# Linear attention and two gated layers on one core: a planner's durations, one new rule of order, and new urgencies

## The chip, the cores and the metric

The kernel runs on one core of a Trainium2 chip. The metric is the device time of one execution in microseconds (us), from the launch to the end of the one program; the median of several executions is quoted. PE is the tensor engine (PEld its weight loads), DVE the vector engine, ACT the scalar engine, SP the engine whose queue issues the DMAs.

## The reference

Three stages follow each other: a linear attention with complex decays (4 batches, 8 heads, 768 tokens, 48 channels a head), a first layer (3072 tokens, 384 to 2048 to 384, with x * sigmoid(1.702 x)), and a second, gated layer (384 to 1536 to 384).

```python
scale = np.minimum(mag, 0.999) / (mag + 1e-06)        # mag = |a|, a = a_re + i a_im
for t in range(S):
    S_re, S_im = ar*S_re - ai*S_im + k_t v_t^T, ar*S_im + ai*S_re
    y[:, :, t] = einsum('bhd,bhde->bhe', q[:, :, t], S_re)
x = y laid out as (tokens, 384)
h = x @ w_in;  x = (h * sigmoid(1.702 h)) @ w_out
g = x @ w_gate;  out = (g * sigmoid(g) * (x @ w_val)) @ w_out2
```

## The kernel before, in words

The attention is done in chunks of 128 tokens; a unit is two chunks of one batch, and there are 12 units. For each unit DVE and ACT compute the decays, their products over the chunk, and the queries and keys with the decays in them. These go to DRAM (tiles dq and dk) and come back with the heads in the partitions (tiles sq and sk). Then PE makes, for each chunk, the scores (sc, 16 products of 128 columns, in two groups of four heads), the results (y, two groups of four heads, line 592 and, from a batch's second chunk on, line 594: products of 48 columns), the change of the state (ds, line 611, 48 columns) and transposes (kt and xp). Units of a batch depend on each other through the state M.

The unit's result xt feeds the first layer: 16 blocks of 128 hidden channels, for each a step of nine products of 256 columns into h (lines 786 to 788), the activation on ACT (line 839 and 841), the rest gs on DVE (line 847), and LAG = 3 blocks later a step of nine such products into acc. These steps of nine are the wide products of the change. All three kinds of wide products are done in three passes, with each operand split in a high and a low part. The second layer works on blocks of 512 tokens with products of 512 and 384 columns (pg, pv and o).

The weights are float64 in DRAM. For each of the 32 blocks of w_in and w_out a row of steps loads the words (line 733), flags the range on ACT (lines 742 and 745), shifts and joins the bits on DVE (lines 750, 753 and 756), rounds to the high part on ACT (line 768), and takes the low part with two products on PE (lines 773 and 774) and a copy on ACT (line 776).

The order of all instructions on all engines is made by a planner at build time (class Plan). Each strand of work is a generator that asks for its next step with an engine and an estimated duration. Plan.run keeps a time at which each engine falls free, takes the steps that could start within 0.02 us of the earliest one, and among them the one with the smallest urgency number; a still more urgent step for the same engine goes first if it could start within a short time (NEAR) of it. The urgency of a step is URGENCY of its kind, plus ten times the unit's place, plus EXTRA for that unit and kind; the weights have W_FIRST + 2 f W_STEP (w_in) and W_FIRST + (2 f + LAG) W_STEP (w_out); the wide products of the first layer have 1000 for all units. A step on ACT that needs another table of functions than the loaded one has TURN added to its urgency. The planned times decide the order alone; on the chip every engine runs its instructions in that order and waits on semaphores.

The kinds of work have letters: a loads the decays' inputs, l loads q, k and v, d the decays, r their root, p the products, k the keys, i the inverse that the keys take (lines 312 and 313), q the queries, s the loads of sq and sk, t the transposes of the keys, h the heads (y and ds), m the scores, x the transposes of the results, g the activations of the first layer.

Of the kernel before, what the change touches and what calls it, by code (L numbers as in the profile page):

```python
# [15 lines left out]
DRAM = bass.MemoryType.DRAM  # L16
# [14 lines left out]
class Slots:  # L31
    """Places for tiles of one tag, with the times at which they fall free."""
# [5 lines left out]
class Plan:  # L38
    """Puts rows of steps in one order for all engines.

    A row (a generator) asks for what its next step needs: (engine, us), an Event, or Slots; it is
    resumed, and then issues the step. Of the steps that could start first, the one of the most
    urgent row is taken. The times are estimates and only the order rests on them.
    """

    # from the end of a step to the start of one that waits for it
    LAT = {"PP": 0.0, "VP": 0.25, "AP": 0.25, "PV": 0.2, "VV": 0.13, "AV": 0.14, "PA": 0.2, "VA": 0.13, "AA": 0.22}
    # some durations (and those of transfers) are taken long: the order then has slack for them
    SLACK = {"A": 1.05, "V": 1.03}

    def __init__(self):
        self.free = dict(P=0.0, V=0.0, A=0.0, S=0.0, D=0.0)
        self.rows = []
        self.now = 0.0
        self.n = 0
        self.warm = 0.0
        self.table = None
        self.row = [0, 0, None, [], None, "S", NEAR]

    def add(self, urgency, gen, after=False, near=None):  # L60
        """A row: its urgency, number, generator, what its next step waits for, that step, and its last step's engine."""
        row = [urgency, self.n, gen, [(self.now, self.row[5])] if after else [], None, "S",
               near or NEAR]
        self.n += 1
        self.rows.append(row)
        self.advance(row, next(gen, None))
# [17 lines left out]
    def rush(self, by):  # L84
        """Makes the row at work more urgent."""
        self.row[0] -= by

    def need(self, nc, table):
        """At the issue of an activation: the table of functions it takes."""
        if self.table != table:  # L90
            nc.scalar.preload_act_table_set(table)
            self.table = table

    def load(self, event, size):
        """After the issue of a transfer of so many bytes."""
        self.free["D"] = max(self.free["D"], self.now + 0.6) + size * 1.3 / 360e3
        self.set(event, self.free["D"] + 3.1 - self.now)
# [9 lines left out]
    def run(self, until=None):  # L107
        while self.rows and (until is None or until.time is None):
# [3 lines left out]
            ready = []  # L112
            for row in self.rows:
                if isinstance(row[4], tuple):
                    turn = row[4][2:] and row[4][2] != self.table
# [6 lines left out]
            if near:  # L122
                row = min(near, key=lambda x: x[1:3])[3]
            engine, us = row[4][:2]
            us *= self.SLACK.get(engine, 1.0)
            # a table of functions is loaded ahead of the step
            start = self.ready(row, SWITCH if row[4][2:] and row[4][2] != self.table else 0.0)
            if engine == "P":
                # the tensor engine's clock is at half speed after a pause
                if start - self.free["P"] > (0.5 if start < self.warm else 2.0):  # L130
                    self.warm = start + 3.4
                if start < self.warm:
                    us *= 2
            self.free[engine] = self.now = start + us
# [5 lines left out]
def vec(n):  # L140
    return "V", 0.065 + n / 960
# [6 lines left out]
def act2(n, *table):  # L148
    """Two, the second on what the first gave."""
    return "A", 0.44 + n / 600, *table  # L150


def pe(n):
    return "P", n


ISSUE = ("S", 0.48)
NEAR = 0.094
SWITCH = 1.3
TURN = 1018.0  # L160
NEAR0 = [0.129, 0.005]
# [3 lines left out]
class Attention:  # L165
    """Linear attention with complex decays, in chunks of 128 tokens.

    With P[t] the product of a chunk's decays up to t, times the phase of all that came before it
    in the batch, q[t] * P[t] and k[s] / P[s] give the chunk's scores by one product, and the state
    passes from chunk to chunk by real factors (powers of two near the chunk's decay; the phase  # L170
    takes up the rest). A unit is a few chunks of a batch. Channels (h, d) lie in the partitions, in
    NT tiles.
    """
# [24 lines left out]
    def start(self, units):  # L198
        """The rows of work of all units: (batch, first chunk, chunks)."""
# [18 lines left out]
    # ---- loads  # L218
# [29 lines left out]
    # ---- decays: a / (|a| + 1e-6) * min(|a|, 0.999)  # L248
    def decays(self, u):
# [11 lines left out]
        # (the logarithm's domain is 2 ** -64 to 2 ** 64)  # L261
# [32 lines left out]
    def root(self, u):  # L294
        """Of the decays' squares."""
        yield u.ev["m2"]
        yield self.slots["r"]
        yield act2(u.F, LN_EXP)
        self.plan.need(self.nc, LN_EXP)
        u.r = self.tile("r", [128, self.NT, u.T])  # L300
        self.nc.scalar.activation(u.r, u.m2, AF.Ln)
        self.nc.scalar.activation(u.r, u.r, AF.Exp, scale=-0.5)
        self.plan.set(u.ev["root"])

    def inverse(self, u):
        """Of the products' squares."""
# [9 lines left out]
    # ---- products of the decays over the chunk  # L316
    def cmul(self, out, x, y, shape):
        """out = x * y over complex pairs [128, 2, *shape] (x and y may be broadcast)."""
# [13 lines left out]
        else:  # L332
            full = [128, 2, 2] + list(shape)
            yield vec(4 * n)
# [12 lines left out]
    def products(self, u, last):  # L347
# [8 lines left out]
        # over the blocks of eight: in fours, then over the fours  # L356
# [13 lines left out]
        # G[.., c] is the phase at the start of chunk c of the unit  # L370
# [10 lines left out]
        # the product up to the start of each block of eight  # L381
# [8 lines left out]
        # joined with the products within the blocks  # L390
# [16 lines left out]
    def passed_on(self, u, G):  # L407
        """The state's factors mag = 1 / kap, powers of two near the unit's decays; the next unit's first phase."""
# [107 lines left out]
    # ---- the heads of a chunk  # L516
# [3 lines left out]
    def turns(self, u):  # L520
        """The keys with the tokens in the partitions."""
# [4 lines left out]
        for c in range(u.n):  # L526
# [3 lines left out]
            for e in range(2):  # L530
                yield slots["m"]
                yield pe(0.36)
# [15 lines left out]
    def masked(self, u, c, g, at):  # L548
        """Scores of four heads, without those that look ahead."""
# [5 lines left out]
        yield pe(0.87)  # L555
# [11 lines left out]
    def heads(self, u, last):  # L567
# [9 lines left out]
        for c in range(u.n):  # L577
# [5 lines left out]
            for g in range(2):  # L583
# [3 lines left out]
                yield pe(0.79 if first else 1.66)  # L587
# [15 lines left out]
            if not final:  # L603
                yield u.turned[c]
                yield slots["m"]
                yield pe(1.29)
# [37 lines left out]
    def turn_x(self, u, c, ysb, turned):  # L644
        """The tokens as columns, in two parts for the products that follow."""
        nc, slots, plan, HD, NT = self.nc, self.slots, self.plan, self.HD, self.NT
        yield slots["m"]
        yield pe(0.38)
# [17 lines left out]
# a unit's urgency is ten times its place, and for each kind of its work:  # L666
URGENCY = dict(a=717.8, d=595, p=-974.9, r=624.6, i=67.1, q=-855.6, k=-193.2, t=-1225.3, h=-1091.9, g=-676.3, s=781.7, l=1191.9, m=-1725.3, x=-1117.4)
RUSH = 1342.0
RUSH2 = 152.5
# [586 lines left out]
```

## Time and profile before

| | |
|---|---|
| median of 3 executions | 1169.94 us |
| lowest and highest | 1165.85 and 1174.10 us |
| span of the profiled execution, first to last instruction | 1167.8 us |
| PE busy | 1096.8 us (94% of the span) |
| DVE busy | 728.8 us (62%) |
| ACT busy | 554.0 us (47%) |

The profiled execution shows its span alone; its own device time is not listed apart from the three. The span is 2.1 us under the median of the three executions and inside their range. A page of the profile gives the busy time of each engine, then the span in 40 equal slices of 29.2 us (each digit the busy share in tenths, 9 for 90% or more; PEclk is the granted TensorE clock, 9 for nearly or fully 2.4 GHz and 5 for half of it).

### The profile page before, as it was taken

The numbers are of one execution on the slowest core, as the hardware profiler recorded it, in microseconds if no ns is written. First come the engines' busy times: TensorE is split into PE (matmuls) and PEld (weight loads), VectorE is DVE, ScalarE is ACT, GpSimd is POOL, SyncE is SP. The second block draws the span as 40 slices with busy tenths as digits, with TensorE's granted clock in tenths as the row PEclk, the third lists the DMA queues.
The fourth block names the chain that finished last, engine by engine and source line by source line (L and its number), as shares of the span: only waits on it lengthen the run. The fifth ranks groups of instructions, "written<-read, shape, count | busy, mean of one in ns | idle before, by whom it ended". The sixth has DMA issues, their size and how long they took to land.

```text
span 1167.8 us, 18608 instructions
## 1 busy us (share of the span) xinstructions
PE 1096.8 (94%) x7312; PEld 1015.9 (87%) x7312; DVE 728.8 (62%) x1638; ACT 554.0 (47%) x1279; POOL 1.1 (0%) x8
## 2 busy tenths in 40 slices
PE   1549899999999999999999999999999999999996
PEld 0228889999999999999999999888888888888886
DVE  6999988889788998888862599622231231322221
ACT  7987545667447656644442699422121121211211
POOL 0000000000000000000000000000000000000000
PEclk9569999999899999999999999999999999999999
DMA  9770715618257263525813664001010010000000
GB/s 329 251 162 15 164 54 136 159 46 150 82 136 135 70 123 95 122 56 109 163 58 72 211 221 145 27 2 54 1 55 1 1 55 1 28 1 1 28 1 30
DMA packets 101391, 103.54 MB, mean 89 GB/s; under 512 B 14001, under 2 KB 95410, under 8 KB 101298
## 3 DMA queue, kind: packets, MB, share of 16 engines
q1 hardware_dynamic: 101298, 102.29, 34.8%
q8 instruction: 59, 0.97, 0.3%
q14 instruction: 34, 0.28, 0.1%
HBM read 73.95 MB, written 28.32 MB: 88 GB/s over the span
## 4 chain that ended last, share of the span: by engine, by line
PE 86%; DMA 7%; DVE 4%; ACT 2%; issue 1%; SPq 0%; DVEq 0%; ACTq 0%
PE h L786 6%; PE h L788 5%; PE h L787 5%; PE acc L786 5%; PE acc L787 5%; PE acc L788 5%; PE o L1005 4%; PE o L1006 4%; PE o L1007 4%; PE pg L787 4%; PE pv L787 4%; PE pv L786 4%; PE pg L788 4%; PE pg L786 4%; PE pv L788 4%; PE sc L559 4%
## 5 line engine op out<-in xcount | busy, mean ns | idle before, releaser
L975 DVE TENSOR_TENSOR s<-s,pv 128x512 f32<-128x512 f32 x72 | 49.5, 687 | 236.0 <-PE pv L788 234.9
L786 PE MATMUL h<-xt,w 128*128 128x256 f32 x576 | 170.0, 295 | 7.8 <-ACT g L841 6.4
L786 PE MATMUL acc<-gs,w 128*128 128x256 f32 x576 | 169.0, 293 | 0.0
L787 PE MATMUL h<-xt,w 128*128 128x256 f32 x576 | 164.8, 286 | 0.6 <-DVE xt L661 0.6
L787 PE MATMUL acc<-gs,w 128*128 128x256 f32 x576 | 164.5, 286 | 0.4 <-DVE gs L847 0.4
L788 PE MATMUL h<-xt,w 128*128 128x256 f32 x576 | 164.5, 286 | 0.0
L788 PE MATMUL acc<-gs,w 128*128 128x256 f32 x576 | 164.5, 286 | 0.0
L839 ACT ACTIVATE gs<-h 128x256 fp32r<-128x256 f32 x192 | 73.8, 384 | 148.7 <-PE h L788 147.3
L972 ACT ACTIVATE s<-pg 128x512 f32<-128x512 f32 x72 | 43.0, 598 | 174.4 <-PE pg L788 174.4
L786 PEld LDWEIGHTS h<-xt,w 128*128 128x128 f32 x576 | 111.8, 194 | 10.8 <-ACT g L841 8.3
L787 PEld LDWEIGHTS h<-xt,w 128*128 128x128 f32 x576 | 111.9, 194 | 1.0 <-DVE xt L661 1.0
L786 PEld LDWEIGHTS acc<-gs,w 128*128 128x128 f32 x576 | 111.9, 194 | 0.7
L787 PEld LDWEIGHTS acc<-gs,w 128*128 128x128 f32 x576 | 111.8, 194 | 0.7 <-DVE gs L847 0.6
L788 PEld LDWEIGHTS h<-xt,w 128*128 128x128 f32 x576 | 111.8, 194 | 0.0
L847 DVE TENSOR_TENSOR gs<-g,gs 128x256 fp32r<-128x256 f32 x192 | 80.6, 421 | 49.8 <-ACT g L841 48.8
L788 PEld LDWEIGHTS acc<-gs,w 128*128 128x128 f32 x576 | 111.6, 194 | 0.0
L980 ACT CAST p<-s 128x512 fp32r<-128x512 f32 x72 | 44.7, 621 | 130.5 <-DVE s L975 130.5
L1005 PE MATMUL o<-w,p 128*128 128x384 f32 x288 | 97.2, 338 | 0.0
L1006 PE MATMUL o<-w,p 128*128 128x384 f32 x288 | 97.2, 337 | 0.0
L1007 PE MATMUL o<-w,p 128*128 128x384 f32 x288 | 97.1, 337 | 0.0
L787 PE MATMUL pg<-xs,w 128*128 128x512 f32 x216 | 85.1, 394 | 0.0
L787 PE MATMUL pv<-xs,w 128*128 128x512 f32 x216 | 84.7, 392 | 0.0
(128 smaller groups left out, 2448.9 us busy)
## 6 DMA issues: line engine op xcount, KB each, us to landing
words<-in_moe_w_out_dram SPq DMA_DIRECT2D x28, 384.0 KB, 8.4
dq<-qh SPq DMA_DIRECT2D x24, 384.0 KB, 8.9
dk<-p SPq DMA_DIRECT2D x24, 384.0 KB, 6.9
sq<-dq SPq DMA_DIRECT2D x24, 384.0 KB, 7.2
sk<-dk SPq DMA_DIRECT2D x24, 384.0 KB, 8.5
words<-in_moe_w_in_dram SPq DMA_DIRECT2D x16, 384.0 KB, 8.4
p<-in_a_re_dram SPq DMA_DIRECT2D x12, 384.0 KB, 3.8
p<-in_a_im_dram SPq DMA_DIRECT2D x12, 384.0 KB, 4.7
```

Of the source, the lines that this page charges most:

```text
L559: T.matmul(sc[:, h], u.sk[:, 4 * g + h, cols(c)], u.sq[:, 4 * g + h, cols(c)], start=True, stop=True)
L786: T.matmul(out, w[:, 0, ws], xh, start=start, stop=False)
L787: T.matmul(out, w[:, 0, ws], xl, start=False, stop=False)
L788: T.matmul(out, w[:, 1, ws], xh, start=False, stop=stop)
L839: A.activation(gs[:, 0], h, AF.Gelu_apprx_sigmoid)
L847: V.tensor_tensor(out=gs[:, 1], in0=g, in1=gs[:, 0].bitcast(F32), op=ALU.subtract)
L972: A.activation(s, gv[0], AF.Silu)
L975: V.tensor_tensor(out=s, in0=s, in1=gv[1], op=ALU.mult)
L980: A.copy(p2[:, 0], s)
L1005: T.matmul(os[i], p2[:, 0, cols(i)], w[:, 0], start=f == 0, stop=False)
L1006: T.matmul(os[i], p2[:, 0, cols(i)], w[:, 1], start=False, stop=False)
L1007: T.matmul(os[i], p2[:, 1, cols(i)], w[:, 0], start=False, stop=f == F2 - 1)
```

## The change

The dataflow, the tiles, the engines of all steps and the number of instructions of each kind stay. Changed are the planner and its numbers, so that the same steps are issued in another order.

- Two groups of products are marked as thin: y (line 592 and 594) and ds (line 611). The planner sums the time of thin steps that follow each other on PE in `few`. If the step it has picked is thin and `few` and this step come over FEW - 0.6 = 2.3 us, it takes in its place the most urgent other PE step that isn't thin and could start within 0.5 us, if there is one.
- The planner's clock of PE is modelled anew: before, half speed for 3.4 us after a pause; now, in fixed stretches of the planned time, half speed in a stretch that follows one with little work, thin steps counted at 0.2.
- Durations: a wide step of nine products 9 (N / 2400 + 0.0135) for 9 N / 2400 + 0.045 (1.08 for 1.00 us at 256 columns); y 1.79 for 1.66 us, ds 1.36 for 1.29, scores 0.90 for 0.87, transposes 0.33 for 0.36 and 0.38, one form of the complex product on DVE 0.3 us longer.
- All urgencies are new numbers: URGENCY, RUSH, RUSH2, EXTRA, NEAR0, W_FIRST, W_STEP and SPILL.

```diff
-            # a table of functions is loaded ahead of the step
-            start = self.ready(row, SWITCH if row[4][2:] and row[4][2] != self.table else 0.0)
+            if row[4][3:] and self.few and self.few + row[4][1] > FEW - 0.6:
+                other = [x for x in ready if x[3][4][0] == "P" and not x[3][4][3:] and x[0] < start + 0.5]
+                if other:
+                    row = min(other, key=lambda x: x[1:3])[3]
...
             if engine == "P":
-                if start - self.free["P"] > (0.5 if start < self.warm else 2.0):
-                    self.warm = start + 3.4
-                if start < self.warm:
+                self.stretch(start)
+                if self.cold:
                     us *= 2
+                thin = row[4][3:]
+                self.few = (self.few if start - self.free["P"] < 0.3 else 0.0) + us if thin else 0.0
+                at = start
+                while at < start + us:
+                    self.stretch(at)
+                    end = min(start + us, (self.part + 1) * STRETCH)
+                    self.work += (end - at) * (0.2 if thin else 1.0)
+                    at = end + 1e-9
...
+    def stretch(self, at):
+        while self.part < int(at / STRETCH):
+            self.cold = self.work < 0.35 * STRETCH
+            self.part += 1
+            self.work = 0.0
...
-            yield vec(4 * n)
+            yield vec(4 * n, 0.3 if n > 48 else 0.0)
...
-                yield pe(0.79 if first else 1.66)
+                yield thin(0.9 if first else 1.79)
...
-                yield pe(1.29)
+                yield thin(1.36)
...
-                yield pe(9 * N / 2400 + 0.045)
+                yield pe(9 * (N / 2400 + MM))
...
+MM = 0.0135
+FEW = 2.9
+STRETCH = 3.413
-NEAR0 = [0.129, 0.005]
+NEAR0 = [0.122, 0.054]
-URGENCY = dict(a=717.8, d=595, p=-974.9, r=624.6, i=67.1, q=-855.6, k=-193.2, t=-1225.3, h=-1091.9, g=-676.3, s=781.7, l=1191.9, m=-1725.3, x=-1117.4)
-RUSH = 1342.0
-RUSH2 = 152.5
+URGENCY = dict(a=717.8, d=727.2, p=-1381.2, r=1320.1, i=1140.8, q=-1417.6, k=-215.1, t=-1308.3, h=-1078.4, g=-1116.1, s=713.6, l=499.3, m=-1658.9, x=-848.6)
+RUSH = 1467.1
+RUSH2 = 315.3
-W_FIRST, W_STEP = 284.7, 16.205
+W_FIRST, W_STEP = 231.0, 8.038
-SPILL = 450.8
+SPILL = 223.6
```

EXTRA has 12 entries, one a unit. Of the first two, the terms that the prediction names: unit 0 a -2878.5, l -411.4, i 214.5 before and a -1741.1, l -876.9, i 961.2 now; unit 1 a -467.2, i -1245.3 before and a -355.5, i 2394.5 now.

## Rows read from the trace of the kernel before

**Rows 1.** The page: busy time, then the span in 40 slices.

```profile
PE 1096.8 (94%) x7312; PEld 1015.9 (87%) x7312; DVE 728.8 (62%) x1638; ACT 554.0 (47%) x1279; POOL 1.1 (0%) x8
PE   1549899999999999999999999999999999999996
DVE  6999988889788998888862599622231231322221
PEclk9569999999899999999999999999999999999999
```

**Rows 2.** Busy time by stage: PE, PEld, DVE, ACT, POOL, clock, DMA share, GB/s.

```profile
0.00:84.20 84.20, 33.28 (x64) 15.14 (x64) 70.71 (x173) 71.81 (x200) 1.14 (x8) 0.68 0.83 250
84.20:142.56 58.36, 53.81 (x392) 48.66 (x392) 55.93 (x142) 38.19 (x87) 0.00 (x0) 0.96 0.44 97
142.56:600.00 457.44, 450.99 (x3777) 447.18 (x3778) 395.77 (x951) 256.95 (x556) 0.00 (x0) 0.97 0.49 107
716.00:1160.00 444.00, 442.72 (x2134) 390.10 (x2132) 134.36 (x220) 114.31 (x217) 0.00 (x0) 1.00 0.05 18
```

**Rows 3.** The same columns in short stretches around a lower clock.

```profile
139.93:143.35 3.42, 1.50 (x12) 1.33 (x12) 1.90 (x6) 0.59 (x2) 0.00 (x0) 0.97 0.94 243
143.35:146.76 3.41, 3.41 (x15) 2.96 (x15) 2.27 (x7) 0.51 (x1) 0.00 (x0) 0.53 0.03 11
...
197.95:201.37 3.42, 3.42 (x33) 3.42 (x31) 3.39 (x5) 1.79 (x3) 0.00 (x0) 0.97 0.00 0
201.37:204.78 3.41, 3.41 (x18) 3.41 (x18) 2.43 (x8) 2.50 (x4) 0.00 (x0) 0.53 0.00 0
...
300.34:303.76 3.42, 3.42 (x20) 3.42 (x19) 1.74 (x2) 1.24 (x4) 0.00 (x0) 0.50 0.00 0
303.76:307.17 3.41, 3.41 (x21) 3.41 (x21) 1.62 (x4) 0.48 (x1) 0.00 (x0) 0.53 0.02 5
...
631.40:634.82 3.42, 3.42 (x20) 3.42 (x19) 0.00 (x0) 0.78 (x3) 0.00 (x0) 0.53 0.00 0
```

**Rows 4.** PE's timeline: start, duration, line, output and inputs, idle time before.

```profile
142.56 3.24 PE L559 MATMUL sc<-sq,sk 96*128 96x128 f32 x16 [1.92 <-DMA sk<-dk]
...
197.93 0.32 PE L592 MATMUL y<-v,at 128*128 128x48 f32 x2
...
201.67 0.56 PE L786 MATMUL h<-xt,w 128*128 128x256 f32 x1
...
208.39 0.39 PE L786 MATMUL h<-xt,w 128*128 128x256 f32 x1 [1.40 <-ACT g L841]
...
302.67 2.68 PE L611 MATMUL ds<-v,kn 128*96 128x48 f32 x16
```

**Rows 5.** The waits by engine and line: total us, times, longest.

```profile
PE h L786 <- ACT g L841: 6.4, 8, 1.4
```

**Rows 6.** The chain that ended last, to 230 us: start, us, what.

```profile
68.89 7.63 DMA dk<-p
76.55 7.52 DMA sk<-dk
...
123.41 11.57 DMA dk<-p
```

**Rows 7.** DVE's groups from 0 to 123 us: count, busy, mean ns.

```profile
L336 DVE TENSOR_TENSOR sp<-p 128x384 f32<-128x384 f32 x17 | 14.6, 856 | 0.1
L756 DVE SCALAR_TENSOR_TENSOR r<-words,r 128x384 int32<-128x384 int32 x26 | 14.3, 550 | 0.0
L282 DVE SCALAR_TENSOR_TENSOR r<-x,r 128x768 f32<-128x768 f32 x3 | 2.8, 949 | 0.0
```

**Rows 8.** ACT's timeline at unit 0's inverse.

```profile
60.51 0.84 ACT L312 ACTIVATE kr<-d 128x768 f32<-128x768 f32 x1 [0.26 <-DVE d L474]
```

**Rows 9.** ACT's groups of the weights from 0 to 84.2 us.

```profile
L742 ACT ACTIVATE junk<-words 128x384 bf16<-128x384 f32 x32 | 17.3, 545 | 1.1 <-DMA words<-in_moe_w_in_dram 1.1
L745 ACT ACTIVATE junk<-junk 128x384 bf16<-128x384 bf16 x32 | 16.5, 519 | 0.0
```

More of the change, by code (lines that the diff above doesn't have):

```diff
@@ L55, in __init__ @@
         self.n = 0
-        self.warm = 0.0
+        self.few = 0.0
+        self.part, self.work, self.cold = 0, 0.0, True
         self.table = None
         self.row = [0, 0, None, [], None, "S", NEAR]
+    def stretch(self, at):
[3 more added lines that the diff above has]
+            self.work = 0.0
     def add(self, urgency, gen, after=False, near=None):
@@ L114, in run @@
                 if isinstance(row[4], tuple):
-                    turn = row[4][2:] and row[4][2] != self.table
+                    turn = row[4][0] == "A" and row[4][2:] and row[4][2] != self.table
                     ready.append((self.ready(row), row[0] + (TURN if turn else 0), row[1], row))
@@ L123, in run @@
                 row = min(near, key=lambda x: x[1:3])[3]
+            if row[4][3:] and self.few and self.few + row[4][1] > FEW - 0.6:
+                other = [x for x in ready if x[3][4][0] == "P" and not x[3][4][3:] and x[0] < start + 0.5]
+                if other:
+                    row = min(other, key=lambda x: x[1:3])[3]
             engine, us = row[4][:2]
             us *= self.SLACK.get(engine, 1.0)
-            start = self.ready(row, SWITCH if row[4][2:] and row[4][2] != self.table else 0.0)
+            start = self.ready(row, SWITCH if engine == "A" and row[4][2:] and row[4][2] != self.table else 0.0)
             if engine == "P":
-                if start - self.free["P"] > (0.5 if start < self.warm else 2.0):
-                    self.warm = start + 3.4
-                if start < self.warm:
+                self.stretch(start)
+                if self.cold:
                     us *= 2
+                thin = row[4][3:]
[6 more added lines that the diff above has]
+                    at = end + 1e-9
             self.free[engine] = self.now = start + us
@@ L137, in run, with vec @@
             self.advance(row, next(row[2], None))
-def vec(n):
-    return "V", 0.065 + n / 960
+def vec(n, more=0.0):
+    return "V", 0.065 + n / 960 + more
 def act(n, more=0.0, *table):
@@ L150, in act2, with thin @@
     return "A", 0.44 + n / 600, *table
+MM = 0.0135
 def pe(n):
     return "P", n
+def thin(n):
+    return "P", n, None, True
 ISSUE = ("S", 0.48)
@@ L531, in turns @@
                 yield slots["m"]
-                yield pe(0.36)
+                yield pe(0.33)
                 if e == 0:
@@ L554, in masked @@
         yield slots["at"]
-        yield pe(0.87)
+        yield pe(0.9)
         plan.rush(RUSH2)
@@ L647, in turn_x @@
         yield slots["m"]
-        yield pe(0.38)
+        yield pe(0.33)
         if c == 0:
@@ L860, in layer_one_out @@
             yield accslots
-        yield pe(9 * N / 2400 + 0.045)
+        yield pe(9 * (N / 2400 + MM))
         if f == 0:
@@ L952, in second @@
                         yield sl
-                        yield pe(9 * N / 2400 + 0.02)
+                        yield pe(9 * (N / 2400 + MM))
                         p = ps.tile([128, N], F32, tag=nm, name=nm)
@@ L998, in second_out @@
                     yield accslots if i == 2 else hslots
-                yield pe(3 * DM / 2400 + 0.005)
+                yield pe(3 * (DM / 2400 + MM))
                 if f == 0 and i < 2:
```

2 lines of the change are left out of this document (1 added, 1 removed).

## The prediction

> **What bounds the kernel now.** I read the page first, for the engine that is nearly always busy [rows 1]. PE is, at 94% of the span, and the slices say where it isn't: in the first three, where DVE and ACT are the full ones, and nearly nowhere after the fourth. The clock row adds a second loss: fives and sixes at the start, and single eights later.
>
> Then the busy time by stage, cut at the first scores of unit 0 (84.2 us) and of unit 1 (142.56 us) [rows 2]. Up to 84.2 us PE works 33.3 us, most of it at half clock, while DVE works 70.7 of 84.2 us. From there to 142.56 us PE works 53.8 of 58.4 us. To 600 us PE lacks only 457.4 - 451.0 = 6.5 us, and in the second layer (716 to 1160 us) 1.3 of 444 us, at full clock. So the second layer can give nothing. What an order of steps can win lies in three places: the start, the 4.6 + 6.5 us of idle PE up to 600 us, and the stretches at half clock.
>
> For those I cut the span into short stretches and looked for a clock under full speed [rows 3]. After 84.2 us there are nine such stretches of 3.4 us; five are among the rows shown. At 201.37 us the clock is 0.53: PE is busy throughout, yet runs 18 products where 33 ran in the stretch before. With the clock half for (1 - 0.53) / 0.5 of 3.41 us, that is 3.2 us, the loss is 1.6 us of work.
>
> PE's timeline says what ran ahead of it [rows 4]. From 197.93 to 201.67 us PE ran one chunk's two groups of y back to back, 3.7 us of products of 48 columns. I counted such pairs, each with both lines 592 and 594: twenty, from 95.07 to 639.83 us. Six of them (at 95, 198, 249, 297, 501 and 628 us) end in half clock, the one at 297 us for two stretches; fourteen do not. The other two stretches follow pauses: the one at 143.35 us comes after a stretch in which PE worked 1.5 of 3.42 us [rows 3], waiting 1.92 us for unit 1's scores [rows 4]; the one at 167 us is of the same kind.
>
> The Trainium skill's page TensorE: Matmul & The Clock Gate (table of two states in "What's actually happening") puts the half rate to idle windows; the trace disagrees for the pairs, whose stretch has PE busy for its full 3.42 us. By the page's rule alone the thin groups would cost no clock, and the first term below would be zero.
>
> **The change, part by part.** *Wide products between thin groups.* After one y (planned 1.79 us) the second would bring the sum to 3.58, over 2.3, so the planner takes another PE step that is ready. In a batch's first chunk it doesn't (0.9 + 0.9). The wide step is moved and not added, so it costs no PE time. What it delays is the second y, the copy of y on ACT, xp, ds and the next state, each by about 1.1 us a chunk; PE has other wide products meanwhile, since it is busy for 451 of 457 us. The cover is gone where a wide step waits for its activation: eight waits of 6.4 us in all, of which the longest, 1.4 us, stands right behind y, ds and a transpose [rows 4, 5]. A wide product spent earlier may make these waits longer or fewer; I take zero, between -6.4 and +6.4 us.
>
> What the rule can win: after 142.56 us five pairs lost six stretches, five at 1.6 us and one, at a clock of 0.50, 1.7 us, and five stretches ahead of them show 0.97, 0.1 us each [rows 3]. Sum 5 x 1.6 + 1.7 + 0.5 = 10.2 us. The sixth pair, at 95 us, lies ahead of the 1.92 us wait at 142.56 us and was hidden by it. The bounds are 0 and -10.2; I take -10, as all other things that follow one y (1.9 us) in this trace, four first chunks among them, kept full clock.
>
> *The start.* Unit 0's keys leave at 68.9 us, come back after 7.6 + 7.5 us, and the scores begin at 84.2; for unit 1 the keys leave at 123.4 us and need 11.6 us and as much again as the second leg takes [rows 6]. PE has no other work of length between these moments than unit 0's: 32 wide steps of 1.08 us and two chunks of thin work. So a shift of unit 0 alone wins nothing: it must then wait for unit 1. Unit 1 is set by DVE, busy nearly throughout from 12 us to 123 us. In that time DVE has finished 26 of the 32 weights, and also work of unit 2: the third of the rows of the decays, five instructions at 0.95 to 1.75 us, together 5.5 us, and three of its 17 large complex products, each 0.86 + 2 x 0.33 us, 4.6 us [rows 7]. About 10 us could therefore go behind unit 1, and that is the end of the gain. Now the numbers: unit 1's input load has rank 717.8 + 10 - 355.5 = 372, so some 17 weights (231 to 368) and q, k and v of unit 0 (-378) go ahead of it on SP's queue; before (261) it went ahead of all weights (285 and more). Its decays then no longer run in the middle of unit 0's chain. But 17 transfers ahead of it also start unit 1 later, by some 18 us of queue, and it must share DVE with more weights. The two pull in opposite ways. I take the smallest gain that needs no luck: the 1.92 us wait at 142.56 us and the half-clock stretch right behind it, 1.6 us, together -3.5 us. The bounds are -10, from the work of unit 2, and +18 from the second rival below.
>
> *Durations.* They have no cost by themselves; they reach the chip through the order alone. The old 0.47 us for a large complex product stood against 0.86 us in the trace [rows 7], the new 0.77 us is nearer, so that the plan for the start rests on better ground. I give this no price of its own.
>
> *Weights.* W_STEP at 8 for 16 puts all weights between 231 and 496, before 285 to 820. After 142.56 us their work is nearly done in either order, so only the start feels it.
>
> **The sum.** 1167.8 - 10 - 3.5 = 1154.3 us of span. The median of the runs lay 2.1 us above the profiled span; I carry that: 1156.4 us, forecast 1156.
>
> **Rivals.** *A: the clock keeps falling.* The step between may be too little: at 300 us PE ran nine wide products between y and ds and the stretch after it was still at half clock, so that ds took 2.68 us [rows 3, 4]. Also the rule takes any step that isn't thin, so a transpose of 0.33 us may stand between two y in place of a wide one. Against it: the wide products there ran after the clock had already fallen. Then only the start remains, 1169.9 - 3.5 = 1166 us.
>
> *B: slower, by the inverse.* The keys of a unit need the inverse on ACT (kind i). Its rank for unit 0 goes from 67.1 + 214.5 = 282, ahead of all weights, to 1140.8 + 961.2 = 2102, behind all of them; for unit 1 from -1168 to 3546. Before, ACT began unit 0's inverse 0.26 us after its input was there [rows 8]. With some ten to twenty weight instructions of 0.55 and 0.52 us [rows 9] standing ready at that moment (I count seven squares and ten of line 745 not yet done at 60.5 us), it would start up to 17 x 0.53 = 9 us later, and unit 1's again. Both lie on the path that sets PE's start: +18 us, less the 10 us of the clock, is 1169.9 + 18 - 10 = 1178 us. What speaks against it is that a less urgent step is still taken when no other could start as early, and that ACT's weight steps wait in turn for DVE. It decides if more than about nine weight instructions on ACT come between the square of unit 0's keys and its inverse in each of the two units: at that point the loss equals the gain of the clock.
>
> *C: the start shortens too.* Unit 2's 10 us on DVE go behind unit 1, unit 0 also comes earlier, and two or three waits for activations vanish: 1169.9 - 10 - 10 - 3 = 1147 us.
>
> *D: by the idle rule of the clock.* Pauses alone would set the clock, so the two stretches after pauses (3.2 us) would go with the pauses and the pairs would keep theirs. The time would be that of A, 1166 us; since the pairs' stretches show no pause, I give it a small part of A's chance. (This is the rule of the page TensorE: Matmul & The Clock Gate in the Trainium skill that was weighed above.)
>
> **How the numbers follow.** The forecast has 0.45, A and D together 0.22 (D 0.04 of it), B 0.13, C 0.20. The range takes the bound of C with one more of the eight activation waits' sum on its side, 1147 - 6.4 = 1141, and on the other side ends at 1176, just short of B's middle, since half of B and a few hundredths of other mishaps may be left out. A measurement of this kernel tells about 1% from no change: its three runs lie within 0.7%. The bounds are 1158.2 and 1181.6 us. Faster by more than 1%: all of C and three quarters of the forecast, 0.54. Slower by more than 1%: a half of B and 0.04 for the unforeseen, 0.10. The rest, 0.36, is within 1%.
>
> **What the profile would show.** If the first term is right, no two groups of y stand back to back with lines 592 and 594, nine wide products lie between, and the stretches of 0.53 after 200 us are gone, with the pairs' 33 products a stretch going on into the next. If the second is right, the scores of unit 1 begin with less than 1.9 us of waiting, and PE idles less than 4.6 us between the two units' first scores. B would show as weight instructions (lines 742 to 776) between the square of unit 0's keys (line 471) and line 312, and first scores of unit 0 after 84 us. The prediction is wrong if half-clock stretches follow y groups that have wide products between them; if DVE's order starves unit 1 or unit 2 so that PE idles by more than 10 us after unit 0; or if the start moves by more than 10 us in either direction.

## The result and the profile after

The changed kernel took 1185.41 us (median of four runs, 1182.61 to 1194.22) beside 1172.02 us of the kernel before (four runs): ratio 1.0144, 95% interval 1.0098 to 1.0191. It is slower by 1.4%, where 1156 us and faster had the most weight. Its profiled execution took 1187.41 us with a span of 1185.4 us, 17.6 us more than before. In the kernel after, 32 is added to the line numbers of before: the scores are line 591, y 624 and 626, ds 643, the wide products 818 to 820.

The page, as [rows 1]: engines, then the span in 40 slices.

```profile
PE 1100.6 (93%) x7312; PEld 1015.0 (86%) x7312; DVE 730.4 (62%) x1638; ACT 554.9 (47%) x1279; POOL 1.1 (0%) x8
PE   3549899988999999999999999999999999999996
DVE  6998889977889897999852689613222222322221
PEclk9988999899999999999999999999999999999999
```

PE is busy 3.8 us longer and idle 84.8 us for 71.0 before (span less busy time). So 13.8 of the 17.6 us are idle time of the engine that bounds the kernel; the eights in its row stand where [rows 1] has nines. Of the 3.8 us more of busy time the scores alone have 3.5 (52.1 us for 48.6): they are the work that follows the waits shown below. The busy time by stage, cut at the first scores of unit 0 (87.6 us) and of unit 1 (138.12 us), columns as in [rows 2]:

```profile
0.00:87.60 87.60, 39.15 (x75) 17.44 (x75) 75.72 (x193) 74.95 (x209) 1.14 (x8) 0.94 0.81 240
87.60:138.12 50.52, 43.99 (x313) 40.00 (x314) 44.74 (x99) 31.71 (x68) 0.00 (x0) 0.93 0.52 108
138.12:600.00 461.88, 447.15 (x3745) 443.24 (x3746) 402.37 (x972) 257.81 (x557) 0.00 (x0) 0.97 0.49 106
716.00:1160.00 444.00, 440.59 (x2143) 387.47 (x2142) 137.33 (x231) 120.10 (x235) 0.00 (x0) 1.00 0.07 23
```

Up to unit 1's scores PE idles 48.45 + 6.53 = 55.0 us, before 50.9 + 4.6 = 55.5 us: no loss and nearly no gain. (The 0.94 of the first row, and the nines that begin the clock row of the page, show no gain in the work: the weights' products, line 805, took 743 ns each, line 773 before 721 ns.) From there to 600 us PE idles 14.7 us for 6.5, in the second layer 3.4 us for 1.3. PE's waits name the cause (total us, times, longest), to be set beside [rows 5]:

```profile
PE sc L591 <- DMA sk<-dk: 12.2, 4, 4.2
PE h L818 <- ACT g L873: 4.5, 5, 1.5
PE o L1037 <- ACT ot L1048: 3.3, 4, 0.8
PE sc L591 <- DMA tots<-md: 2.8, 2, 2.6
```

The scores wait 15.0 us for transfers (keys sk, factors tots), before 2.2 us; o, which did not wait before, waits 3.3 us for the copies of the results; the waits for activations are shorter than before (6.4). In PE's timeline, as [rows 4], the longest wait of the scores for each of units 1, 3 and 4, and one of the four of o:

```profile
138.12 1.16 PE L591 MATMUL sc<-sq,sk 96*128 96x128 f32 x6 [3.48 <-DMA sk<-dk]
...
240.10 2.91 PE L591 MATMUL sc<-sq,sk 96*128 96x128 f32 x16 [4.24 <-DMA sk<-dk]
...
292.42 3.76 PE L591 MATMUL sc<-sq,sk 96*128 96x128 f32 x16 [3.06 <-DMA sk<-dk]
...
883.64 0.44 PE L1037 MATMUL o<-w,p 128*128 128x384 f32 x1 [0.82 <-ACT ot L1048]
```

The chain that ended last passes through these transfers, as in [rows 6] (start, us, what):

```profile
119.02 11.33 DMA dk<-p
130.37 7.62 DMA sk<-dk
...
219.09 10.42 DMA dk<-p
229.57 10.39 DMA sk<-dk
239.96 0.14 issue
240.10 2.91 PE sc L591 x16
```

One leg of the keys takes 7.6 to 11.3 us here. The planner's price for it, from Plan.load, is 786432 bytes x 1.3 / 360e3 + 3.1 = 5.9 us, counted from 0.6 us after the planned issue where no earlier transfer is under way, so 6.5 us from the issue; each unit's keys make two legs. The factors tots, 1.5 KB, have no bytes in their price: 0.6 + 3.1 us. From issue to landing they took 9.7 us in the median (5.2 before):

```profile
tots<-md SPq DMA_DIRECT2D x16, 1.5 KB, 9.7
```

While PE stands at 240 us, wide products of earlier units follow in its order, but PE takes its instructions in order.

Behind these waits the clock falls. Short stretches as in [rows 3]:

```profile
201.37:204.78 3.41, 3.41 (x32) 3.41 (x31) 3.38 (x6) 3.33 (x7) 0.00 (x0) 1.00 0.00 0
238.91:242.32 3.41, 2.22 (x14) 2.25 (x15) 0.80 (x2) 0.00 (x0) 0.00 (x0) 0.81 0.76 260
242.32:245.74 3.42, 3.42 (x24) 3.42 (x23) 1.73 (x8) 0.66 (x2) 0.00 (x0) 0.69 0.01 3
290.10:293.52 3.42, 1.10 (x5) 1.14 (x6) 0.41 (x1) 0.00 (x0) 0.00 (x0) 0.81 1.07 284
293.52:296.93 3.41, 3.41 (x18) 3.41 (x18) 1.65 (x4) 0.00 (x0) 0.00 (x0) 0.50 0.21 74
296.93:300.34 3.41, 3.41 (x23) 3.41 (x23) 2.98 (x7) 0.00 (x0) 0.00 (x0) 0.69 0.02 5
```

The new rule did its work: 18 of the 20 pairs of y are apart, 17 with a wide step between them and one with the products of a weight, and the stretch at 201.37 us, at 0.53 before, is at full clock. But twelve of the stretches so cut after 123 us are below it: nine behind the waits for scores at 138, 240, 292 and 452 us, three behind one of the two pairs left together, at 213 us, and two short waits (0.67 and 0.57 us) for its copies. Summing (1 - granted clock) x length over stretches of 3.41 us from 123 to 641 us (standing time counted too) gives 13.6 us before and 11.9 us after: the half clock was moved, not removed.

### The profile page after: what moved, and what is told of

The parts are those of the page before. It is cut to its first block, busy times and chain, and to the rows that moved or that the text cites. A ratio compares the mean times of both kernels' runs of the same rounds, so it can differ in the third digit from the quotient of the medians.

```text
span 1185.4 us, 18605 instructions
## 1 busy us (share of the span) xinstructions
PE 1100.6 (93%) x7312; PEld 1015.0 (86%) x7312; DVE 730.4 (62%) x1638; ACT 554.9 (47%) x1279; POOL 1.1 (0%) x8
## 4 chain that ended last, share of the span: by engine, by line
PE 74%; DMA 12%; DVE 8%; ACT 4%; issue 2%; SPq 0%; DVEq 0%; ACTq 0%
DMA dk<-p 4%; PE h L818 4%; PE o L1037 4%; PE acc L818 4%; PE pg L819 4%; PE o L1039 4%; PE pg L820 4%; PE pg L818 4%; PE o L1038 4%; PE acc L819 4%; PE h L820 4%; PE pv L819 4%; PE h L819 4%; PE acc L820 4%; PE pv L818 4%; PE pv L820 4%
## 5 line engine op out<-in xcount | busy, mean ns | idle before, releaser
L805 PE MATMUL h<-r,ident 128*128 128x384 f32 x64 | 41.5, 743 | 47.6 <-DVE r L788 46.6
```

Source lines behind the costliest of these rows:

```text
L805: T.matmul(p, at.ident, r, start=True, stop=False)
```

## The experiments

Names of theories in the expectations: R, the rule holds the clock and is worth about what the first term said; N, it is worth nothing; S, the loss comes from scores placed ahead of their keys, since transfers are priced too short; U, it comes from the new urgencies. In the first two expectations, split_in_old_order and joined_in_new_order, the letters stand for something else: S there says that the rule gives the clock back and the loss is in new waits, and R that the rule itself costs. Since the median of the kernel before differs from chip to chip (1172 to 1182 us), ratios are compared. "Keys" is the time that scores waited, nearly all of it for transfers, "ot" that o waited for its copy; "idle" is PE's from 123 to 641 us, "clock" the sum of the paragraph above (from 123 to 641 us), all in us from the one execution that was profiled. Such sums differ between executions of one order: the kernel after and after_old_second_layer have the same order on PE up to 600 us, and waited 15.0 and 17.7 us.

| run | ratio (95% interval) | span | keys | ot | idle | clock |
|---|---|---|---|---|---|---|
| before | 1 | 1167.8 | 2.2 | 0 | 9.3 | 13.6 |
| after | 1.0144 (1.0098 to 1.0191) | 1185.4 | 15.0 | 3.3 | 18.2 | 11.9 |
| split_in_old_order | 1.0075 (1.0038 to 1.0112) | 1176.8 | 9.0 | 0 | 19.9 | 8.6 |
| joined_in_new_order | 1.0246 (1.0192 to 1.0300) | 1201.1 | 18.4 | 3.3 | 22.2 | 25.6 |
| wide_ahead_of_scores | 1.0272 (1.0218 to 1.0326) | 1204.1 | 4.2 | 3.3 | 30.5 | 15.4 |
| rule_alone | 1.0131 (1.0072 to 1.0189) | 1190.2 | 9.5 | 0 | 18.9 | 27.3 |
| new_urgencies_old_planner | 1.0159 (1.0103 to 1.0215) | 1194.7 | 8.9 | 0 | 21.6 | 22.2 |
| old_urgencies_new_planner | 1.0093 (1.0060 to 1.0126) | 1184.2 | 12.7 | 3.3 | 20.0 | 15.3 |
| long_transfers | 1.0060 (1.0026 to 1.0094) | 1179.7 | 0 | 10.9 | 8.5 | 0.3 |
| after_old_second_layer | 1.0094 (1.0064 to 1.0124) | 1183.0 | 17.7 | 0 | 20.7 | 11.9 |
| long_transfers_old_second | 0.9920 (0.9892 to 0.9947) | 1164.5 | 0 | 0 | 8.5 | 0.0 |
| late_plan_joined | 1.0022 (0.9992 to 1.0051) | 1174.8 | 0 | 0 | 10.5 | 8.5 |
| late_plan_rule_off | 1.0019 (0.9986 to 1.0053) | 1181.1 | 0 | 0 | 11.0 | 13.4 |
| late_plan_old_urgencies | 0.9895 (0.9858 to 0.9931) | 1163.4 | 0 | 0 | 8.4 | 4.5 |
| late_plan_half_way | 1.0005 (0.9973 to 1.0037) | 1183.4 | 2.2 | 0 | 15.4 | 17.1 |
| before_long_transfers | 1.0065 (1.0038 to 1.0093) | 1186.7 | 0 | 0 | 12.7 | 21.0 |
| after_short_wide_steps | 1.0106 (1.0064 to 1.0148) | 1192.7 | 10.7 | 0 | 25.6 | 17.1 |

### The rule, by moving single steps

**split_in_old_order.** The order of the kernel before, step for step, with the next wide step pulled between the two groups of y in 19 of 20 chunks.

```diff
 order on PE, one chunk
-y (heads 0-3)  y (heads 4-7)  wide step  xp  ds
+y (heads 0-3)  wide step  y (heads 4-7)  xp  ds
```

> The kernel before, all its steps in its own order, but in 19 of its 20 pairs of y groups the next wide step of the first layer is put between the two groups. Nothing else moves. Theory S (the rule gives back the clock that pairs cost; the changed kernel loses by waits that the new order brings in): five pairs after 142 us cost six half-clock stretches, so 8 to 10 us less than before, a ratio of 0.991 to 0.993, and no half-clock stretch behind a y group that stands apart. Theory R (the rule itself costs, since it delays every chunk's y, ds and state by a wide step): equal or slower, ratio 1.000 to 1.010.

A miss for S, and inside the range of that expectation's R: 0.75% slower. Two waits in PE's list grew:

```profile
PE sc L629 <- DMA sk<-dk: 6.5, 2, 4.9
PE xp L724 <- ACT ysb L669: 5.4, 8, 0.7
```

The wide step behind the second y had been the cover of ACT's copy ysb; spent earlier, it left xp to wait 0.7 us in eight chunks, and y and ds side by side. And the clock did fall behind groups that stand apart, against the last part of S: at 257, 499 and 643 us PE ran y, a wide step, y, waited 0.67 us and went on with xp and ds. In the timeline, and then in the short stretches:

```profile
255.94 0.44 PE L724 MATMUL xp<-ident,ysb 128*128 128x128 f32 x2 [0.67 <-ACT ysb L669]
...
255.99:259.40 3.41, 3.41 (x24) 3.41 (x25) 1.57 (x4) 3.29 (x7) 0.00 (x0) 0.64 0.02 5
```

So a wide step between two groups does not always hold the clock. In these three chunks a short wait and thin work stand behind the second group, where the kernel after mostly has another wide step; that this makes the difference is not shown.

**joined_in_new_order.** The order of the kernel after, with the wide step of 16 split pairs put behind the second group: the same edit backwards.

```diff
-y (heads 0-3)  wide step  y (heads 4-7)
+y (heads 0-3)  y (heads 4-7)  wide step
```

> The changed kernel, all its steps in its own order, but in 16 of the 18 pairs that the rule had taken apart the wide step goes back behind the second y group. Theory S: pairs fall into half clock again as in the kernel before, about 6 in 20, so some five more stretches at 1.6 us: 6 to 10 us slower than the changed kernel, 1191 to 1196 us. Theory R: 5 to 10 us faster than the changed kernel, 1176 to 1181 us.

Slower than after by 1.0 percentage points, some 12 us, more than the 6 to 10 us expected; clock loss 25.6 for 11.9 us. The waits for keys grew too, by 3.4 us, so not all of it is clock. Inside the new order the rule is worth about the 10 us of the prediction. So the loss of the change lies elsewhere.

**wide_ahead_of_scores.** In the kernel after, 4, 4, 4, 2 and 4 wide steps of earlier units, with their activations, moved ahead of the first scores of units 1, 3, 4, 6 and 7.

```diff
-scores of unit u  wide steps of unit u - 1
+2 or 4 wide steps of unit u - 1  scores of unit u  the others
```

> The changed kernel, but ahead of the first scores of units 1, 3, 4 and 7 four more wide steps are put, and two ahead of those of unit 6; they come from behind these units' chunks, with their activations, and keep their own order. Theory S (PE waits there in its order for keys that are still on their way, with wide steps ready behind the scores): the waits of 3.5, 4.2, 3.1, 1.5 and 2.6 us and some 6 us of half clock behind them go, about 20 us: 1164 to 1174 us. Theory U (the new urgencies make the units' keys late, so that PE lacks work in any case): the waits come back at the end of the moved steps, later or at the next unit; 1180 us or more.

A miss: 1.3 percentage points slower than after. The waits for keys fell to 4.2 us as meant, but activations and DVE steps, moved with their products, came late in turn:

```profile
PE h L873 <- ACT g L928: 19.5, 13, 6.0
PE acc L874 <- DVE gs L934: 6.9, 3, 4.6
```

An order cannot be mended in five places by hand; what follows plans it anew.

### Which part of the change makes the waits

**rule_alone.** The kernel before with the rule and the thin marks, its old durations, clock and urgencies.

```diff
+            if row[4][3:] and self.few and self.few + row[4][1] > FEW - 0.6:
+                other = [x for x in ready if x[3][4][0] == "P" and not x[3][4][3:] and x[0] < start + 0.5]
+                if other:
+                    row = min(other, key=lambda x: x[1:3])[3]
...
-                yield pe(0.79 if first else 1.66)
+                yield thin(0.79 if first else 1.66)
```

> The kernel before, planned anew with the thin rule alone: old durations, old urgencies, old clock model. If the rule pays by itself: no half clock behind y groups after 200 us, 4 to 9 us less, ratio 0.992 to 0.997. If it only moves the cost (as the split in the fixed order did, where xp stood right behind the second y and waited 0.67 us for ACT's copy eight times, and y and ds came together): ratio 1.000 to 1.008.

**new_urgencies_old_planner.** The kernel before with the new numbers alone, **old_urgencies_new_planner** the kernel after with the old ones.

```diff
-URGENCY = dict(a=717.8, d=595, p=-974.9, r=624.6, i=67.1, ...
+URGENCY = dict(a=717.8, d=727.2, p=-1381.2, r=1320.1, i=1140.8, ...
-W_FIRST, W_STEP = 284.7, 16.205
+W_FIRST, W_STEP = 231.0, 8.038
```

> The kernel before with the new urgencies (URGENCY, RUSH, RUSH2, EXTRA, NEAR0, W_FIRST, W_STEP, SPILL) alone: old durations, old clock model, no rule. Theory S (the planner with PE priced as measured and transfers priced too short puts scores ahead of their keys): the old, short PE prices let the chip run behind the plan, so the scores wait for sk and tots less than 6 us in all; ratio to before 0.995 to 1.008. Theory U (the new urgencies make the keys late): waits of the scores over 10 us and a ratio of 1.010 or more.

> The changed kernel with the urgencies of before: new durations, new clock model and the rule. Theory S: scores wait for sk and tots 8 us or more in all, and the ratio to before is 1.008 or more. Theory U: waits under 5 us and a ratio of 1.000 or less.

All three are 0.9 to 1.6% slower than before, and all wait 9 to 13 us ahead of scores. rule_alone missed both of its ranges. new_urgencies_old_planner went against S (8.9 us of waits where S allowed 6, ratio 1.0159 where S allowed 1.008): it has the ratio of U, and waits just under U's. old_urgencies_new_planner went with S. The rule alone or the urgencies alone are enough for such waits, and they stay without the new urgencies; so they hang on no one of these parts, and each new plan with the short price of transfers has them. The new clock model has no run of its own.

### The price of transfers

**long_transfers.** The kernel after, planned with 3 us more for each transfer (8.9 us for a leg of the keys).

```diff
-        self.set(event, self.free["D"] + 3.1 - self.now)
+        self.set(event, self.free["D"] + 6.1 - self.now)
```

> The changed kernel, planned anew with one number changed: every transfer is taken to end 6.1 us in place of 3.1 us after its bytes are through. Theory S (the planner prices PE as measured now, but still prices a transfer at 5.9 us a leg where the keys' legs take 7.6 to 11.3 us, so its scores stand too early): waits of the scores for sk below 4 us in all, where the changed kernel has 15; 1160 to 1176 us. Theory U: the keys come as late as before, the waits are over 10 us in all and the time is 1180 us or more. The start may move by some us either way in both, since all is planned anew.

The waits for keys are gone, and with them the half clock from 123 to 641 us (0.3 us left). But the waits for ot grew to 10.9 us, five of 2.19 us each, and behind three of the five the clock falls in the second layer too, which the table's sum leaves out (5.1 us more):

```profile
800.00:1140.00 340.00, 331.25 (x1567) 290.38 (x1567) 80.76 (x115) 71.97 (x116) 0.00 (x0) 0.98 0.04 15
```

In its waits S holds; in time it missed (1182.44 us, where it allowed 1160 to 1176). It is 0.6% slower than before, 0.8 points better than after.

**after_old_second_layer.** The kernel after with the second layer's products priced as before.

```diff
-                        yield pe(9 * (N / 2400 + MM))
+                        yield pe(9 * N / 2400 + 0.02)
...
-                yield pe(3 * (DM / 2400 + MM))
+                yield pe(3 * DM / 2400 + 0.005)
```

> The kernel after with the second layer's products of PE priced as in the kernel before (1.94 and 0.485 us) and nothing else changed, so that the part up to 660 us is the same. If the new prices there cost the four waits of o for its copy (3.3 us) and nothing else, the time is 3 to 4 us under that of the kernel after, ratio to before about 1.011, and the waits of o for ot are gone. If these waits come from the other order of the first layer, they stay and the time is that of the kernel after.

The waits for ot are gone, and the span is 2.4 us shorter; the ratio fell by half a point, but the two intervals overlap. So those waits came from the new durations of the second layer.

**long_transfers_old_second.** Both edits, the long price up to the end of the attention and the first layer only.

```diff
-        self.set(event, self.free["D"] + 3.1 - self.now)
+        self.set(event, self.free["D"] + self.late - self.now)   # 6.1, later 3.1
...
     plan.run(at.done)
+    plan.late = 3.1
     heads.close()
```

> The changed kernel with transfers taken 3 us longer up to the end of the attention, and the second layer's PE steps priced as before. Theory S, with the second layer's order as a second cause: no wait of o for the copies of the results (10.9 us with the long transfers alone, 3.3 us in the changed kernel), waits for sk still below 4 us, so 1168 to 1174 us, ratio to before 0.992 to 1.000. Against it: if the waits for the copies were hidden by others, 1178 us or more.

1166.51 us, ratio 0.992: the first version that beats the kernel before, and a little more than expected. No score waits for a transfer, and no stretch after 123 us is below full clock. Its start is later than that of either kernel (first scores at 97.6 us, 84.2 before): unit 0's scores were not what bounds the start. Its ten executions lie between 1166.03 and 1167.95 us, where nineteen of the kernel before on the same chip spread from 1166.15 to 1183.50 us: the fastest of before are as fast. That fits pairs which lose the clock in some executions and not in others, but only one execution of the kernel before was traced, so this is not shown.

**late_plan_half_way.** The same with 4.6 for 6.1.

> The source of the run long_transfers_old_second with 4.6 in place of 6.1 as the end of a transfer's price, half way to the 3.1 of the kernel after. By S the waits of the scores for their keys come back in part, 3 to 10 us, each with half clock behind it: 1169 to 1178 us. If any longer price does, it is at 1164 to 1169 us with no such waits.

1179.35 us, just past the end of what S allowed, though the waits for keys are only 2.2 us, under its 3 to 10. The profiled execution, 1185.35 us, is one of the slowest of twelve. Its longest wait shows why, in PE's timeline and then in the short stretches:

```profile
281.25 1.91 PE L592 MATMUL sc<-sq,sk 96*128 96x128 f32 x15 [1.61 <-DMA sk<-dk]
```

```profile
279.87:283.28 3.41, 2.02 (x17) 2.06 (x18) 3.18 (x7) 2.96 (x8) 0.00 (x0) 0.97 0.73 212
283.28:286.69 3.41, 3.41 (x19) 3.41 (x17) 3.34 (x8) 1.41 (x2) 0.00 (x0) 0.50 0.41 140
286.69:290.10 3.41, 3.41 (x17) 3.41 (x17) 1.26 (x3) 0.27 (x1) 0.00 (x0) 0.50 0.01 2
290.10:293.52 3.42, 3.42 (x19) 3.42 (x17) 2.19 (x3) 0.66 (x2) 0.00 (x0) 0.50 0.02 5
293.52:296.93 3.41, 3.41 (x19) 3.41 (x19) 1.21 (x3) 0.86 (x3) 0.00 (x0) 0.50 0.00 0
296.93:300.34 3.41, 3.41 (x21) 3.41 (x21) 1.50 (x5) 0.48 (x1) 0.00 (x0) 0.53 0.00 0
```

A wait of 1.61 us is followed by five stretches at half clock, (4 x 0.50 + 0.47) x 3.41 = 8.4 us, with PE busy throughout. The scores and y groups that follow have one wide step between them, which kept the clock up elsewhere; here it did not bring it back.

**before_long_transfers.** The long price in the kernel before, without rule or new durations.

> The kernel before, planned anew with its own urgencies, prices and clock, where only a transfer counts 3 us longer (6.1 for 3.1) up to the end of the first layer. The kernel before waits only some 2 to 4 us for keys. If waits for keys are what the price of transfers takes away and the half clock behind pairs stays (R with S), it wins at most these and their half clock: 1166 to 1176 us, pairs still followed by half clock. If the longer price alone makes a fast plan (N), it comes to 1160 us or less.

0.65% slower, past what R with S allowed, with no wait for keys and 21.0 us of clock loss: behind six of its 20 pairs, one of them right after a wait of 3.6 us for DVE and 8.5 us of the loss, and once behind a wait of 2.1 us for an activation. The price alone gives nothing; what the rule adds to it, the next two runs show.

### The rule again, where nothing waits for keys

**late_plan_joined** is the order of long_transfers_old_second with the 19 split pairs joined, **late_plan_rule_off** its source planned with the rule off.

```diff
-FEW = 2.9
+FEW = 1e9
```

> The order of the run long_transfers_old_second (1166.5 us, no waits for keys, no half clock behind 123 us), with the wide step between the two groups of y put behind the second group in all 19 split pairs; nothing else moves. If the rule of thin groups holds the clock (theory R), stretches at half clock come back behind some six to ten of the pairs, at 1.6 us each, and nothing else changes much: 1174 to 1182 us. If the rule is worth nothing and the whole gain came from the price of the transfers (theory N), there is no half clock after 123 us and the time is 1164 to 1169 us.

> The source of the run long_transfers_old_second, planned anew with the rule switched off (FEW so high that it never applies); prices and urgencies stay. The planner then leaves 19 pairs side by side. By R some pairs lose the clock, 8 to 16 us: 1174 to 1183 us, with few waits of the scores for their keys. By N 1164 to 1169 us.

Both are 1.0 percentage points, some 12 us, behind long_transfers_old_second, inside what R expects; N falls. Of the five falls of the clock in late_plan_joined four stand behind joined pairs, fewer than R's six to ten, and one behind a wait of 2.4 us for an activation; in late_plan_rule_off it is seven of eight. The same moment in both orders, first late_plan_joined, whose two groups of y run from 294.29 us on without a pause:

```profile
293.52:296.93 3.41, 3.41 (x33) 3.41 (x32) 3.38 (x6) 0.00 (x0) 0.00 (x0) 1.00 0.00 0
296.93:300.34 3.41, 3.41 (x23) 3.41 (x23) 0.53 (x3) 0.57 (x3) 0.00 (x0) 0.68 0.02 5
```

and long_transfers_old_second, where a wide step lies between:

```profile
296.93:300.34 3.41, 3.41 (x33) 3.41 (x32) 2.78 (x8) 2.93 (x8) 0.00 (x0) 1.00 0.02 5
300.34:303.76 3.42, 3.42 (x36) 3.42 (x34) 3.42 (x7) 3.36 (x5) 0.00 (x0) 1.00 0.15 49
```

### Two questions left

**late_plan_old_urgencies.** long_transfers_old_second with all urgencies of the kernel before.

> The source of the run long_transfers_old_second with all urgencies and their kin (URGENCY, RUSH, RUSH2, EXTRA, NEAR0, W_FIRST, W_STEP, SPILL) of the kernel before. If prices and rule make the fast plan (S), the time is 1162 to 1173 us, with no waits for keys. If the new urgencies carry the gain (theory U), waits of other kinds appear (activations, DVE) and the time is 1176 us or more.

0.9895, its interval overlapping that of long_transfers_old_second: in time U falls. Of the waits that U named, those for ACT are there, 8.0 us in two, and behind the longer one, 5.6 us, 3.4 of the run's 4.5 us of clock loss. It is the fastest ratio of the study, 1167.62 us beside 1181.63 us of the kernel before on that chip.

**after_short_wide_steps.** The kernel after with the wide steps priced as before, to see whether the measured price had taken away a slack.

```diff
-                yield pe(9 * (N / 2400 + MM))
+                yield pe(9 * N / 2400 + 0.045)
```

> The kernel after, planned anew with a wide step of the first layer (and a product step pg or pv of the second) priced as in the kernel before (1.005 for 1.08 us). If the measured price took away the slack that covered too short transfers (theory S), the chip again runs behind the plan by 0.075 us a wide step and the waits of the scores for their keys and factors, 20 us in all in the kernel after, fall below 10 us; time 1170 to 1180 us. If the slack was never in PE's prices, the waits stay at 14 us or more and the time is 1182 us or more.

The waits fell only from 15.0 to 10.7 us (the expectation's 20 us was too high a count), PE's idle time rose from 18.2 to 25.6 us, and the time stayed above that of before. This part of S is not borne out: why the kernel before, with the same short price, waits only 2.2 us stays open.

## Why the prediction was wrong, point by point

**The step that failed is what the new order was taken to cost: no waits but the activations'.** It stands at two places of the prediction. Of the step that is moved it says that it "costs no PE time", and takes zero for the activation waits that may change, "between -6.4 and +6.4 us"; of the durations it says "I give this no price of its own". The scores' waits for their keys behind unit 1 have no term, and the side of loss is rival B alone. The runs showed these waits in its place. PE's 13.8 us more of idle time are 12.8 us of waits of scores for transfers, 3.3 us of waits of o, and 2.3 us less elsewhere; and behind the waits the half clock came back, so that on balance 1.7 of the 10.2 us of the first term were left. The waits for keys hang on no single part of the change: they come with the rule alone (9.5 us) and with the urgencies alone (8.9 us), both with the old durations. Only the waits of o hang on the durations, those of the second layer. The number that would have told it stood in [rows 6]: legs of 7.63, 7.52 and 11.57 us against a price of 5.9 us (6.5 from the issue) in Plan.load, which the change leaves as it was. Shown by long_transfers (no waits for keys, no half clock up to 641 us), long_transfers_old_second (0.992) and before_long_transfers (not the price alone). Over all runs that were planned anew, scores waited 0 in each of the five with 3 us more a transfer, 2.2 us in the one half way, and 8.9 to 17.7 us in each of the six with the short price. The kernel before has the short price too and waits 2.2 us; why stays open.

**Wide products between thin groups, -10 us: the mechanism was right, and the size about right**, where nothing else brings the clock down: about 12 us in late_plan_joined, whose trace has 8.5 us of clock loss, four fifths of it behind pairs. That 10.2 came so close has some luck in it: it is the loss of one execution, and those of the kernel before lie up to 17 us apart on one chip. Half clock behind pairs without any pause is shown; by the idle rule of rival D it would not be there. (The Trainium skill's page TensorE: Matmul & The Clock Gate, table of two states in "What's actually happening", puts the half rate to idle windows: half clock behind the waits goes its way in part, though PE worked 2.22 of the 3.41 us at 238.91 us; the stretch at 296.93 us of late_plan_joined, busy for all of its 3.41 us, disagrees.) Costing the moved step at nothing because "PE has other wide products meanwhile" was wrong as an argument: in split_in_old_order the moved step was the cover of ACT's copy, 5.4 us of new waits. The kernel after's own plan kept that cover.

**The start, -3.5 us: it gave 0.5 us of idle time and no clock.** Unit 1's scores began 4.4 us earlier, but waited 3.48 us for 1.92, and half clock follows as before. That a shift of unit 0 alone wins nothing held: the best plans begin it at 86.6 and 97.6 us.

**"The second layer can give nothing"** held for gains only: the new durations there put result copies behind other work on ACT, 3.3 us, and none with the old prices.

**The rivals.** A, in part: one wide step between held the clock in long_transfers_old_second; in split_in_old_order, with a short wait and thin work behind, it didn't in three chunks, and after a pause it did not bring it back (late_plan_half_way). B had the right sign by another mechanism. Its late inverse is there, as against [rows 8]: the input was ready at 58.17 + 0.95 = 59.1 us, and ACT, working through weights, came to it at

```profile
66.65 0.86 ACT L344 ACTIVATE kr<-d 128x768 f32<-128x768 f32 x1
```

7.5 us late. Yet unit 0's scores came 3.4 us later and unit 1's earlier, and PE's idle time up to there fell. C did not happen. Of the signs, "the prediction is wrong if DVE's order starves unit 1 or unit 2" looked at the wrong place: transfers starved units 1, 3, 4, 6 and 7. (In B the new rank of unit 1's inverse is 1140.8 + 10 + 2394.5 = 3545, not 3546; nothing hangs on it.)

## What to carry to other kernels

When a planner's prices are corrected, compare all of them with the trace, those that the change leaves alone too: one that stays too short can place steps ahead of their data on an in-order engine. Ask of a wide step that is to be moved what it hides where it stands. And judge a rule of order in a plan that has no other waits: here it was worth 1%, and lay hidden under waits of the same size.

## What the runs showed of the hardware

A short wait ahead of thin work can cost several times itself: in one execution 1.61 us of waiting were followed by 8.4 us of clock loss (late_plan_half_way), with PE busy and one wide step between the thin groups. Each of the waits of 2.6 to 4.2 us in the kernel after is followed by 3.4 to 6.8 us at half clock. The same wait can go either way: of five waits of 2.19 us ahead of o in long_transfers, the clock fell behind three. A round trip leg of 768 KB through DRAM took between 7.4 and 11.6 us in the chains of the two kernels, and one price for it is either too short for some or too long for the rest.
